# Bucket rows loaded transposed, expert rows added into the output by accumulating scatters

## The chip, the core and the metric

One core of a Trainium2 chip runs the whole kernel in one launch. The metric is the device time of that launch in microseconds (us).

## The reference

Block-wise causal attention (batch 8, 8 heads, 576 tokens, head size 64, blocks of 64), then a mixture of 8 experts with noisy top-2 routing over the 4608 tokens of 512 values. Cut to what matters:

```python
scores = np.where(block_i >= block_j, scale * q @ k.T, -1e9)
x = softmax(scores) @ v                       # (4608, 512)
noisy = x @ w_gate + log1p(exp(x @ w_noise)) * noise
top2_w = softmax(top 2 of noisy)              # per token
for e in range(8):
    for k in range(2):
        mask = top2[:, k] == e
        out[mask] += top2_w[mask, k, None] * (relu(x[mask] @ w1[e]) @ w2[e])
```

## The kernel before

Attention runs over four groups `g` of two batches, each nine row tiles of 128 tokens. For each group q and k are loaded and transposed on TensorE, scores and exponentials are made in two sets of four heads, and the result lands in `xr` (128 x 9 x 512, BF16). A router then finds each token's two experts and its place in their buckets. Two groups make a half; each half has its own bucket array `xd` in HBM, 8 experts x 640 rows, which a store from the tile `zero` clears at the start (unused rows must be finite). For each of the 72 pairs of row tile and choice, GpSimd scatters 128 rows of `xr` into `xd` at `slots`.

The expert stage takes 16 steps, half 0 and then half 1, experts 0 to 7 in each. `load_x` brings a bucket (640 x 512) into `xg` on SyncE's queue, two steps ahead. `expert` transposes it on TensorE into `xgT` (20 transposes and 4 VectorE copies), makes `hp` = w1 x `xgT` (64 matmuls), passes it through a Relu on ScalarE into `hsb`, makes `yp` = `hsb` x w2 in five row tiles (40 matmuls), copies each to `ysb` and stores it to `yd` in HBM. After the eighth and after the last step `combine` gathers, for each of 18 row tiles, the two expert rows of each token from `yd` (GpSimd, `gslots`), weighs and adds them (VectorE, `wts`) and stores to `out`.

Order: a framework places the instructions. Each engine gets its list in an order fixed before the run, by a model in which, of the instructions that are ready, the one that comes first in the program goes first; each tile waits for those that lay in its place. The second pool block lies over the first, in the order of its pools: `wL` (6 experts x 16 KB a partition), `xg`, `xgT`, `hsb` (2 x 10 KB), `ysb`, `fin`. In the first block `raw`, `qk`, `v` and the exponentials end at 124,448 bytes, and the two `xr` follow, to 142,880. Weights of experts 0 and 1 have a pool of their own; those of 2 to 7 are loaded into `wL` by GpSimd's queue.

After the last step a branch, not taken with this input, handles buckets that overflow.

Of the kernel before, what the change touches and what calls it, by code (L numbers as in the profile page):

```python
# [8 lines left out]
F32 = mybir.dt.float32  # L9
# [10 lines left out]
def kernel(  # L20
# [29 lines left out]
    NW = CAP // 2  # L50
    OVB = E * CAP
    XR = OVB + 2 * TH * P
    BIG = float(1 << 20)
    SET = 4
    EO = (0, 576, 1024, 1344)
    ESC = 1536
    scale = 1.0 / (D ** 0.5)

    xd = [nc.dram_tensor(f"xd{i}", (XR, Dm), BF16, kind="Internal").ap() for i in range(NH)]
    yd = [nc.dram_tensor(f"yd{i}", (OVB, Dm), BF16, kind="Internal").ap() for i in range(NH)]  # L60

# [25 lines left out]

    nz_all = keep.tile([P, NT, E], F32)
    slots = keep.tile([P, NT, 2], I32)
    gslots = keep.tile([P, NT, 2], I32)  # L90
    wts = keep.tile([P, 2, NT], F32)
    oh_all = keep.tile([P, NG, 2, E, TG], BF16)
    zero = keep.tile([P, 2048], BF16)

    def setup_consts():
        make_identity(nc, ident_f)
        nc.vector.tensor_copy(ident, ident_f)
        nc.gpsimd.memset(prem, 0.0)
        nc.gpsimd.affine_select(out=prem, in_=prem, compare_op=ALU.is_gt, fill=-1.0,
                                base=0, pattern=[[1, P]], channel_multiplier=-1)  # L100
        nc.vector.memset(ones_mat, 1.0)
        nc.gpsimd.iota(ecap_i, pattern=[[CAP, E], [0, 1]], base=0, channel_multiplier=0)
        nc.vector.tensor_copy(ecap, ecap_i)
        nc.vector.memset(rmask, 1.0)
        nc.vector.memset(rmask[:, :, 0:1], 0.0)
        nc.gpsimd.iota(ovrow_i, pattern=[[TH * P, 2], [P, TH]], base=OVB, channel_multiplier=1)
        nc.vector.tensor_copy(ovrow, ovrow_i)
        for i in range(NH):
            nc.vector.memset(base[i], 0.0)

    wload = {}

# [14 lines left out]
    with tc.tile_pool(name="raw", bufs=2) as raw_pool, \  # L127
# [59 lines left out]

        nc.vector.memset(zero, 0.0)
        for i in range(NH):
            zr = OVB // P  # L190
            nc.sync.dma_start(
                out=xd[i][0:OVB, :].rearrange("(p a) d -> p (a d)", p=P).rearrange("p (a c) -> p a c", c=2048),
                in_=zero.unsqueeze(1).to_broadcast([P, zr * Dm // 2048, 2048]))
# [8 lines left out]
        for g in range(NG):  # L202
# [12 lines left out]
                load_w(wE, 0)  # L215
                load_w(wE, 1)

            xr = xr_pool.tile([P, TG, Dm], BF16, tag="xr")
# [126 lines left out]
            for i in range(2):  # L345
# [4 lines left out]
            nc.vector.tensor_scalar(gslots[:, t0:t0 + TG, :].rearrange("p t i -> p i t"), sl2,  # L350
                                    float(OVB - 1), None, op0=ALU.min)
            nc.vector.tensor_copy(slots[:, t0:t0 + TG, :].rearrange("p t i -> p i t"), sl2)  # L352


            for idx in range(TG):
                for i in range(2):
                    ins = nc.gpsimd.indirect_dma_start(  # L357
                        out=xd[half], out_offset=bass.IndirectOffsetOnAxis(
                            ap=slots[:, t0 + idx, i:i + 1], axis=0),
                        in_=xr[:, idx, :], in_offset=None,  # L360
                        bounds_check=XR - 1, oob_is_err=False)
                    key = f"scat{half}"
                    tc.declare_no_dep(ins.ins, group=key, reason="rows of one half are distinct") if scat[half] else None
                    tc.add_to_no_dep_group(key, ins.ins)
                    scat[half].append(ins.ins.name)


    with tc.tile_pool(name="wL", bufs=1) as wL, \
         tc.tile_pool(name="xgp", bufs=3) as xg_pool, \
         tc.tile_pool(name="xgtp", bufs=2) as xgt_pool, \  # L370
# [5 lines left out]
         tc.tile_pool(name="ft_ps", bufs=2, space=PSUM) as ft_ps:  # L376

        def load_x(half, e):
            xg = xg_pool.tile([P, CT, Dm], BF16, tag="xg")
            ins = nc.sync.dma_start(out=xg, in_=xd[half][e * CAP:(e + 1) * CAP, :]  # L380
                                    .rearrange("(c p) d -> p c d", p=P))
            for nm in scat[half]:
                tc.add_manual_dep(ins.ins, nm, SYNC_DEP, reason="rows landed")
            return xg

        def expert(half, e, xg):
            w1sb, w2sb = wload[e]
            xgT = xgt_pool.tile([P, DB, CAP], BF16, tag="xgT")
            for db in range(DB):
                tp = ft_ps.tile([P, CAP], BF16, tag="ft")  # L390
                for c in range(CT):
                    nc.tensor.transpose(tp[:, c * P:(c + 1) * P], xg[:, c, db * P:(db + 1) * P], ident)  # L392
                nc.vector.tensor_copy(xgT[:, db, :], tp)  # L393
            hsb = h_pool.tile([P, FB, CAP], BF16, tag="hsb")
            for fb in range(FB):
                hp = hp_ps.tile([P, 2, 512], F32, tag="hp")
                for db in range(DB):
                    for n in range(2):
                        nc.tensor.matmul(out=hp[:, n, 0:NW], lhsT=w1sb[:, db, fb * P:(fb + 1) * P],  # L399
                                         rhs=xgT[:, db, n * NW:(n + 1) * NW],  # L400
                                         start=(db == 0), stop=(db == DB - 1))
                nc.scalar.activation(out=hsb[:, fb, :].rearrange("p (n w) -> p n w", n=2),  # L402
                                     in_=hp[:, :, 0:NW], func=AF.Relu)
            for c in range(CT):
                yp = yp_ps.tile([P, Dm], F32, tag="yp")
                for fb in range(FB):
                    nc.tensor.matmul(out=yp, lhsT=hsb[:, fb, c * P:(c + 1) * P], rhs=w2sb[:, fb, :],  # L407
                                     start=(fb == 0), stop=(fb == FB - 1))
                ysb = y_pool.tile([P, Dm], BF16, tag="ysb")
                nc.vector.tensor_copy(ysb, yp)  # L410
                nc.sync.dma_start(out=yd[half][e * CAP + c * P:e * CAP + (c + 1) * P, :], in_=ysb)

        def combine(half):
            for tl in range(TH):
                t = half * TH + tl
                g, idx = divmod(t, TG)
                yg = fin.tile([P, 2, Dm], BF16, tag="yg")
                for i in range(2):
                    nc.gpsimd.indirect_dma_start(  # L419
                        out=yg[:, i, :], out_offset=None, in_=yd[half],  # L420
                        in_offset=bass.IndirectOffsetOnAxis(ap=gslots[:, t, i:i + 1], axis=0),
                        bounds_check=OVB - 1, oob_is_err=False)
                acc = fin.tile([P, Dm], F32, tag="acc")
                nc.vector.tensor_scalar(acc, yg[:, 0, :], wts[:, 0, t:t + 1], None, op0=ALU.mult)  # L424
                nc.vector.scalar_tensor_tensor(out=acc, in0=yg[:, 1, :], scalar=wts[:, 1, t:t + 1], in1=acc,  # L425
                                               op0=ALU.mult, op1=ALU.add)
                for p0, n, tok in token_rows(g, idx):
                    nc.sync.dma_start(out=out[tok:tok + n, :], in_=acc[p0:p0 + n, :])

        seq = [(half, e) for half in range(NH) for e in range(E)]  # L430
        xgs = {0: load_x(*seq[0]), 1: load_x(*seq[1])}
        for e in range(2, E):
            load_w(wL, e)
        for i, (half, e) in enumerate(seq):
            if i + 2 < len(seq):
                xgs[i + 2] = load_x(*seq[i + 2])
            expert(half, e, xgs.pop(i))
            if i == E - 1:
                combine(0)
        combine(1)  # L440

# [10 lines left out]
        with tc.If(over > 0):  # L452
# [15 lines left out]
            for half in range(NH):  # L468
                with tc.For_i(half * TH * P, (half + 1) * TH * P, P) as r0:
# [4 lines left out]
                    xo = fin.tile([P, 2, Dm], BF16, tag="yg")  # L474
                    nc.gpsimd.indirect_dma_start(
                        out=xo[:, 0, :], out_offset=None, in_=xd[half],
                        in_offset=bass.IndirectOffsetOnAxis(ap=sidx, axis=0),
                        bounds_check=XR - 1, oob_is_err=False)
                    tp = ft_ps.tile([P, CAP], BF16, tag="ft")
                    for db in range(DB):  # L480
                        nc.tensor.transpose(tp[:, db * P:(db + 1) * P], xo[:, 0, db * P:(db + 1) * P], ident)
# [50 lines left out]
```

## Time and profile before

| | |
|---|---|
| median of 3 runs | 726.08 us (724.75 to 729.91) |
| profiled execution | 728.31 us, of which the span is 726.5 us |
| TensorE, share of the span | 65% (472.7 us) |
| VectorE, ScalarE, GpSimd | 35%, 26%, 30% |
| DMA | 91.62 MB, 102,902 packets |
| mean granted clock of TensorE | 0.785 of full speed |

A share of the span says little here, since the stages have different limits: loads at the start, attention, experts, combine. A stage is read by the stretch of time that it takes, and a wait by what released it. L399 in a row is line 399 of the kernel before. q0 is the DMA queue of GpSimd, q1 the queues of SyncE and ScalarE.

### The profile page before, as it was taken

To read this page: it belongs to the slowest core of one execution; us is meant where nothing else is said; L and a number is where in the kernel's file an instruction comes from. 1 tells how busy PE (TensorE), PEld (TensorE's weight loads), DVE (VectorE), ACT (ScalarE), POOL (GpSimd) and SP (SyncE) were. 2 spreads that over 40 slices of the span, in tenths; PEclk is the share of its full clock that TensorE was granted. 3 is DMA by queue.
4 is the path that set the end of the run, shared out by engine and by line. 5 is a ranking of instruction groups with operands and counts; after the bars stand their busy time and mean duration, and the time that the engine had idled before them with its cause. 6 is when DMAs were issued, how large, how long until landed. Compare 5 with 4: busy or idle time off the path is not lost.

```text
span 726.5 us, 10418 instructions
## 1 busy us (share of the span) xinstructions
PE 472.7 (65%) x4264; PEld 292.6 (40%) x4264; DVE 253.3 (35%) x591; ACT 187.3 (26%) x245; POOL 218.7 (30%) x244
## 2 busy tenths in 40 slices
PE   2087788361786284039999999964179999996000
PEld 1045446130563163025555555541055555553000
DVE  3054946150474155002222222235332222221443
ACT  0084480160415130013322222230033322221000
POOL 5126625777004413370000000077600000001773
PEclk9988866555566566559999999995589999999555
DMA  9999999492001209969942212256432221111564
GB/s 207 343 231 169 181 195 177 142 124 101 1 2 60 73 15 260 210 133 221 226 125 73 71 55 59 72 176 200 150 105 73 73 73 37 37 37 46 177 192 146
DMA packets 102902, 91.62 MB, mean 126 GB/s; under 512 B 49088, under 2 KB 86976, under 8 KB 102848
## 3 DMA queue, kind: packets, MB, share of 16 engines
q0 software_dynamic: 67744, 49.84, 45.8%
q1 hardware_dynamic: 35104, 41.05, 17.7%
q8 instruction: 35, 0.57, 0.3%
q14 instruction: 19, 0.16, 0.1%
HBM read 81.97 MB, written 39.85 MB: 168 GB/s over the span
## 4 chain that ended last, share of the span: by engine, by line
PE 50%; issue 12%; DMA 9%; another core or an unknown queue 9%; POOL 7%; DVE 7%; ACT 6%; POOLq 0%; DVEq 0%; ACTq 0%; SPq 0%
PE hp L399 18%; PE yp L407 18%; ACT esc L237 6%; POOL yg L419 4%; DMA kr<-in_k_dram 4%; PE av L261 4%; DMA vt<-in_v_dram 3%; PE sc L233 2%; PE av L275 2%; POOL xd L357 2%; PE tp L392 2%; PE tp L166 2%; DVE ysb L410 1%; PE tp L288 1%
## 5 line engine op out<-in xcount | busy, mean ns | idle before, releaser
L399 PE MATMUL hp<-xgT,w 128*128 128x320 bf16 x1024 | 149.9, 305 | 33.6 <-ACT hsb L402 33.6
L419 POOL DMA_INDIRECT yg<-yd,gslots x72 | 75.6, 1050 | 317.6 <-PE hp L399 149.4
L402 ACT ACTIVATE hsb<-hp 128x640 bf16<-128x640 f32 x128 | 89.9, 703 | 288.7 <-PE hp L399 246.6
L407 PE MATMUL yp<-w,hsb 128*128 128x512 bf16 x640 | 146.4, 388 | 17.8 <-DVE ysb L410 14.8
L399 PEld LDWEIGHTS <-w 128*128 128x128 bf16 x1024 | 101.5, 100 | 74.8 <-issue 34.0
L410 DVE CAST ysb<-yp 128x512 bf16<-128x512 f32 x80 | 55.3, 691 | 212.3 <-PE yp L407 203.3
L237 ACT ACTIVATE esc<-sc 128x1024 bf16<-128x1024 f32 x96 | 91.5, 1036 | 127.8 <-PE sc L233 72.2
L407 PEld LDWEIGHTS <-hsb 128*128 128x128 bf16 x640 | 63.5, 99 | 94.5 <-issue 24.5
L357 POOL DMA_INDIRECT xd<-xr,slots x72 | 71.0, 986 | 92.8 <-DVE slots L352 46.9
L233 PE MATMUL sc<-qT,kT 64*128 64x512 bf16 (+4 forms) x320 | 52.8, 376 | 29.4 <-ACT esc L237 27.4
L261 PE MATMUL av<-vt,esc 128*128 128x65 bf16 x640 | 42.6, 234 | 38.5 <-DVE xr L279 29.7
L261 PEld LDWEIGHTS <-esc 128*128 128x128 bf16 x640 | 34.4, 123 | 52.9 <-DVE xr L279 35.1
L155 POOL DMA_DIRECT2D vt<-in_v_dram x40 | 33.7, 867 | 53.6 <-DMA kr<-in_k_dram 14.2
L392 PE MATMUL tp<-ident,xg 128*128 128x128 bf16 x320 | 27.7, 233 | 28.5 <-DVE xgT L393 24.6
L393 DVE COPY xgT<-tp 128x640 bf16<-128x640 bf16 x64 | 29.0, 486 | 47.9 <-PE hp L399 44.8
L392 PEld LDWEIGHTS <-xg 128*128 128x128 bf16 x320 | 23.0, 105 | 35.8 <-DVE xgT L393 17.6
L278 DVE RECIPROCAL rden<-av 128x4 f32<-128x4 f32 x72 | 13.0, 182 | 68.1 <-remote 41.7
L166 PE MATMUL tp<-ident,qr 128*64 128x128 bf16 (+1 forms) x320 | 18.8, 274 | 27.2 <-DMA qr<-in_q_dram 14.8
L233 PEld LDWEIGHTS <-kT 64*128 64x128 bf16 x320 | 15.1, 102 | 51.5 <-issue 47.2
L172 DVE COPY qT<-tp 128x1024 bf16<-128x1024 bf16 (+1 forms) x20 | 22.3, 1117 | 33.8 <-PE tp L166 20.3
L425 DVE SCALAR_TENSOR_TENSOR acc<-yg,wts,acc 128x512 f32<-128x512 bf16 x36 | 26.5, 748 | 17.8 <-DMA yg<-yd,gslots 17.7
L424 DVE TENSOR_SCALAR acc<-yg,wts 128x512 f32<-128x512 bf16 x36 | 19.0, 529 | 35.8 <-DMA yg<-yd,gslots 31.1
(78 smaller groups left out, 278.9 us busy)
## 6 DMA issues: line engine op xcount, KB each, us to landing
w<-in_moe_w_dram POOLq DMA_DIRECT2D x16, 1024.0 KB
xd<-zero SPq DMA_DIRECT2D x2, 5120.0 KB
xg<-xd SPq DMA_DIRECT2D x16, 640.0 KB
yd<-ysb SPq DMA_DIRECT2D x80, 128.0 KB
out_dram<-acc SPq DMA_DIRECT2D x32, 256.0 KB
vt<-in_v_dram POOLq DMA_DIRECT2D x32, 128.0 KB
qr<-in_q_dram POOLq DMA_DIRECT2D x8, 384.0 KB
kr<-in_k_dram POOLq DMA_DIRECT2D x8, 384.0 KB
```

The lines of the kernel that those rows point to most:

```text
L155: nc.gpsimd.dma_start(out=vb[p0:p0 + n, idx, :, 0:D], in_=v[b, :, s0:s0 + n, :].rearrange("h s d -> s h d"))
L166: nc.tensor.transpose(tp[64 * hf:64 * hf + 64, r * n:(r + 1) * n], raw[p0:p0 + n, src_t, r * 64:(r + 1) * 64], ident[p0:p0 + n, p0:p0 + n])
L233: nc.tensor.matmul(out=sc[:, hf, off:off + z - a], lhsT=kT[sl, c0 + jt * P:c0 + jt * P + P], rhs=qT[sl, c0 + a:c0 + z], start=True, stop=True)
L237: nc.scalar.activation(out=esc[:, hh, :, u * 512:(u + 1) * 512], in_=sc, func=AF.Exp, scale=scale)
L261: nc.tensor.matmul(out=av[:, hh, :], lhsT=esc[:, hh, hf, c:c + P], rhs=vb[:, 4 * hf + jt, h, :], start=(jt == 0), stop=(jt == ib))
L357: ins = nc.gpsimd.indirect_dma_start(out=xd[half], out_offset=bass.IndirectOffsetOnAxis(ap=slots[:, t0 + idx, i:i + 1], axis=0), in_=xr[:, ...
L392: nc.tensor.transpose(tp[:, c * P:(c + 1) * P], xg[:, c, db * P:(db + 1) * P], ident)
L399: nc.tensor.matmul(out=hp[:, n, 0:NW], lhsT=w1sb[:, db, fb * P:(fb + 1) * P], rhs=xgT[:, db, n * NW:(n + 1) * NW], start=(db == 0), stop=( ...
L402: nc.scalar.activation(out=hsb[:, fb, :].rearrange("p (n w) -> p n w", n=2), in_=hp[:, :, 0:NW], func=AF.Relu)
L407: nc.tensor.matmul(out=yp, lhsT=hsb[:, fb, c * P:(c + 1) * P], rhs=w2sb[:, fb, :], start=(fb == 0), stop=(fb == FB - 1))
L410: nc.vector.tensor_copy(ysb, yp)
L419: nc.gpsimd.indirect_dma_start(out=yg[:, i, :], out_offset=None, in_=yd[half], in_offset=bass.IndirectOffsetOnAxis(ap=gslots[:, t, i:i + 1 ...
```

## The change

`load_x` loads each bucket transposed by the DMA itself, into a tile of the shape of `xgT`; the 20 transposes and the copies of `expert` are gone, and so is the pool of `xgT`. `yd`, `gslots` and `combine` are gone. Each bucket row has 8 more BF16 places, a record of four words: its slot, its token (as 8192 minus the token, so that an unused row, which is zero, points past the end), the second weight, and the first minus the second. `load_rec` reads the records of a half back, once, and makes of them for each bucket row the token number and the weight. `expert` scales each row of `yp` by its weight into an F32 `ysb` and adds it into `out` by an accumulating scatter from GpSimd; `out` is cleared by a store on ScalarE's queue. The first scatter of an expert waits for those of the expert before it, the other four don't.

```diff
+    DR = Dm + 8
+    TOKM = 8192
...
-    xd = [nc.dram_tensor(f"xd{i}", (XR, Dm), BF16, kind="Internal").ap() for i in range(NH)]
-    yd = [nc.dram_tensor(f"yd{i}", (OVB, Dm), BF16, kind="Internal").ap() for i in range(NH)]
+    xd = [nc.dram_tensor(f"xd{i}", (XR, DR), BF16, kind="Internal").ap() for i in range(NH)]
...
-    zero = keep.tile([P, 2048], BF16)
+    zero = keep.tile([P, 2080], BF16)
...
+            rec = xr[:, :, Dm:DR]
+            nc.vector.tensor_copy(rec[:, :, 0:2].bitcast(F32)[:, :, 0], sl2[:, 0, :])
+            nc.vector.tensor_copy(rec[:, :, 2:4].bitcast(I32)[:, :, 0], tokm[:, g, :])
+            nc.vector.tensor_copy(rec[:, :, 4:6].bitcast(F32)[:, :, 0], wk[:, 1, :])
+            nc.vector.tensor_tensor(out=rec[:, :, 6:8].bitcast(F32)[:, :, 0], in0=wk[:, 0, :],
+                                    in1=wk[:, 1, :], op=ALU.subtract)
...
         def load_x(half, e):
-            xg = xg_pool.tile([P, CT, Dm], BF16, tag="xg")
-            ins = nc.sync.dma_start(out=xg, in_=xd[half][e * CAP:(e + 1) * CAP, :]
-                                    .rearrange("(c p) d -> p c d", p=P))
+            xg = xg_pool.tile([P, DB, CAP], BF16, tag="xg")
+            ins = nc.sync.dma_start_transpose(out=xg, in_=xd[half][e * CAP:(e + 1) * CAP, 0:Dm])
...
-            xgT = xgt_pool.tile([P, DB, CAP], BF16, tag="xgT")
-            for db in range(DB):
-                tp = ft_ps.tile([P, CAP], BF16, tag="ft")
-                for c in range(CT):
-                    nc.tensor.transpose(tp[:, c * P:(c + 1) * P], xg[:, c, db * P:(db + 1) * P], ident)
-                nc.vector.tensor_copy(xgT[:, db, :], tp)
...
-                ysb = y_pool.tile([P, Dm], BF16, tag="ysb")
-                nc.vector.tensor_copy(ysb, yp)
-                nc.sync.dma_start(out=yd[half][e * CAP + c * P:e * CAP + (c + 1) * P, :], in_=ysb)
-
-        def combine(half):
...
+                ysb = y_pool.tile([P, Dm], F32, tag="ysb")
+                nc.vector.tensor_scalar(ysb, yp, wrow[half][:, e, c:c + 1], None, op0=ALU.mult)
+                ins = nc.gpsimd.indirect_dma_start(
+                    out=out, out_offset=bass.IndirectOffsetOnAxis(ap=trow[half][:, e, c:c + 1], axis=0),
+                    in_=ysb, in_offset=None, bounds_check=N - 1, oob_is_err=False, compute_op=ALU.add)
+                key = f"acc{half}_{e}"
+                if c:
+                    tc.declare_no_dep(ins.ins, group=key, reason="tokens of one expert are distinct")
+                tc.add_to_no_dep_group(key, ins.ins)
...
+        def load_rec(half):
+            rc = fin.tile([P, E, CT, 4], I32, tag="rc", bufs=1)
+            ins = nc.sync.dma_start(out=rc.rearrange("p e c w -> p (e c) w"),
+                                    in_=xd[half].bitcast(I32)[0:OVB, Dm // 2:DR // 2]
+                                    .rearrange("(c p) w -> p c w", p=P))
...
+            nc.vector.tensor_scalar(tr, f[1], -1.0, float(TOKM), op0=ALU.mult, op1=ALU.add)
...
         xgs = {0: load_x(*seq[0]), 1: load_x(*seq[1])}
+        load_rec(0)
+        zf = zero[:, 0:2048].bitcast(F32)
+        nc.scalar.dma_start(out=out.rearrange("(p a) d -> p (a d)", p=P).rearrange("p (a c) -> p a c", c=1024),
+                            in_=zf.unsqueeze(1).to_broadcast([P, N * Dm // P // 1024, 1024]))
         for e in range(2, E):
             load_w(wL, e)
...
             expert(half, e, xgs.pop(i))
-            if i == E - 1:
-                combine(0)
-        combine(1)
+            if i == 0:
+                load_rec(1)
```

## Rows read from the trace of the kernel before

**Rows 1.** The page, part 2, forty slices of 18.2 us: TensorE busy, granted clock

```profile
PE   2087788361786284039999999964179999996000
...
PEclk9988866555566566559999999995589999999555
```

**Rows 2.** Table of stretches: length, busy time of each engine, clock, DMA share, GB/s

```profile
0.00:35.00 35.00, 5.57 (x83) 3.91 (x83) 7.48 (x18) 1.28 (x1) 13.18 (x25) 1.00 1.00 271
35.00:57.00 22.00, 17.69 (x249) 10.38 (x251) 11.25 (x25) 17.19 (x19) 6.78 (x10) 0.84 1.98 230
...
290.00:320.00 30.00, 0.27 (x2) 0.16 (x2) 0.00 (x0) 1.03 (x2) 15.80 (x18) 0.50 0.72 171
...
375.00:471.00 96.00, 92.99 (x617) 56.28 (x615) 25.36 (x45) 28.13 (x40) 0.00 (x0) 1.00 0.22 69
471.00:532.00 61.00, 26.29 (x136) 14.01 (x136) 27.48 (x49) 5.62 (x8) 38.30 (x36) 0.68 0.56 177
...
667.00:726.50 59.50, 0.00 (x0) 0.00 (x0) 22.66 (x36) 0.00 (x0) 37.28 (x36) 0.53 0.52 162
```

**Rows 3.** The chain of waits at the start: start us, us, what

```profile
6.21 29.41 DMA kr<-in_k_dram
35.91 19.55 DMA vt<-in_v_dram
```

**Rows 4.** Timeline of one steady expert: start us, us, engine, line, operation

```profile
392.60 0.72 PE L392 MATMUL tp<-ident,xg 128*128 128x128 bf16 x10
392.80 0.69 DVE L410 CAST ysb<-yp 128x512 bf16<-128x512 f32 x1 [1.03 <-PE yp L407]
...
394.63 8.78 PE L399 MATMUL hp<-xgT,w 128*128 128x320 bf16 x63
...
403.25 8.80 PE L407 MATMUL yp<-w,hsb 128*128 128x512 bf16 x40
...
411.89 0.72 PE L392 MATMUL tp<-ident,xg 128*128 128x128 bf16 x10
```

**Rows 5.** Timeline where the expert stage starts; idle time and its releaser in brackets

```profile
298.49 0.98 POOL L357 DMA_INDIRECT xd<-xr,slots  x1 [5.53 <-DMA w<-in_moe_w_dram]
...
316.40 0.98 POOL L357 DMA_INDIRECT xd<-xr,slots  x1 [0.30 <-issue]
317.37 0.84 POOL L115 DMA_DIRECT2D w<-in_moe_w_dram  x1
...
318.97 1.30 ACT L402 ACTIVATE hsb<-hp 128x640 bf16<-128x640 f32 x2 [39.55 <-DMA xd<-xr,slots]
...
323.09 0.97 POOL L117 DMA_DIRECT2D w<-in_moe_w_dram  x1
```

**Rows 6.** DMA queues, 10 to 15 us: packets, MB, share of 16 engines

```profile
q1 hardware_dynamic: 330, 1.35, 70.7%
```

**Rows 7.** DMA queues, 278 to 280 us

```profile
q0 software_dynamic: 158, 0.32, 84.9%
q1 hardware_dynamic: 153, 0.16, 28.2%
```

**Rows 8.** DMA queues, 50 to 55 us: the noise loads

```profile
q1 hardware_dynamic: 1012, 0.03, 39.4%
```

**Rows 9.** DMA queues, 320 to 375 us: weights of experts 4 to 7

```profile
q0 software_dynamic: 6220, 8.28, 85.9%
```

**Rows 10.** DMA queues, 667 to 726 us: the gathers of the last combine

```profile
q0 software_dynamic: 1728, 4.72, 29.3%
```

**Rows 11.** Timeline, order of issue at the start and after the last router

```profile
0.75 3.25 SPq L200 DMA_DIRECT2D nz_all<-in_moe_noise_dram  x7
...
4.04 1.38 SPq L191 DMA_DIRECT2D xd<-zero  x2
...
283.95 0.23 DVE L446 TENSOR_REDUCE cmax<-base 128x1 f32<-128x8 f32 x2
```

**Rows 12.** Timeline, the last instruction of VectorE

```profile
719.56 0.75 DVE L425 SCALAR_TENSOR_TENSOR acc<-yg,wts,acc 128x512 f32<-128x512 bf16 x1 [1.30 <-DMA yg<-yd,gslots]
```

More of the change, by code (lines that the diff above doesn't have):

```diff
@@ L89 @@
     slots = keep.tile([P, NT, 2], I32)
-    gslots = keep.tile([P, NT, 2], I32)
     wts = keep.tile([P, 2, NT], F32)
+    tokm = consts.tile([P, NG, TG], I32)
+    rowid_i = consts.tile([P, E, CT], I32)
+    rowid = consts.tile([P, E, CT], F32)
     oh_all = keep.tile([P, NG, 2, E, TG], BF16)
-    zero = keep.tile([P, 2048], BF16)
+    zero = keep.tile([P, 2080], BF16)
     def setup_consts():
@@ L109, in setup_consts @@
             nc.vector.memset(base[i], 0.0)
+        nc.gpsimd.iota(tokm[:, :, 0:8].rearrange("p g (b t) -> p g b t", b=2),
+                       pattern=[[-2 * S, NG], [-S, 2], [-P, 4]], base=TOKM, channel_multiplier=-1)
+        for hf in range(2):
+            nc.gpsimd.iota(tokm[64 * hf:64 * hf + 64, :, 8:9], pattern=[[-2 * S, NG], [0, 1]],
+                           base=TOKM - 512 - hf * S, channel_multiplier=-1)
+        nc.gpsimd.iota(rowid_i, pattern=[[CAP, E], [P, CT]], base=0, channel_multiplier=1)
+        nc.vector.tensor_copy(rowid, rowid_i)
     wload = {}
@@ L189 @@
         for i in range(NH):
-            zr = OVB // P
             nc.sync.dma_start(
-                out=xd[i][0:OVB, :].rearrange("(p a) d -> p (a d)", p=P).rearrange("p (a c) -> p a c", c=2048),
-                in_=zero.unsqueeze(1).to_broadcast([P, zr * Dm // 2048, 2048]))
+                out=xd[i][0:OVB, :].rearrange("(p a) d -> p (a d)", p=P).rearrange("p (a c) -> p a c", c=2080),
+                in_=zero.unsqueeze(1).to_broadcast([P, OVB * DR // P // 2080, 2080]))
         load_v(0)
@@ L216 @@
                 load_w(wE, 1)
-            xr = xr_pool.tile([P, TG, Dm], BF16, tag="xr")
+            xr = xr_pool.tile([P, TG, DR], BF16, tag="xr")
             for st in range(H // SET):
@@ L349 @@
             nc.vector.tensor_tensor(out=sl2, in0=sl2, in1=ovrow[:, :, tl:tl + TG], op=ALU.min)
-            nc.vector.tensor_scalar(gslots[:, t0:t0 + TG, :].rearrange("p t i -> p i t"), sl2,
-                                    float(OVB - 1), None, op0=ALU.min)
             nc.vector.tensor_copy(slots[:, t0:t0 + TG, :].rearrange("p t i -> p i t"), sl2)
+            rec = xr[:, :, Dm:DR]
[4 more added lines that the diff above has]
+                                    in1=wk[:, 1, :], op=ALU.subtract)
             for idx in range(TG):
@@ L357 @@
                     ins = nc.gpsimd.indirect_dma_start(
-                        out=xd[half], out_offset=bass.IndirectOffsetOnAxis(
+                        out=xd[half].bitcast(I32), out_offset=bass.IndirectOffsetOnAxis(
                             ap=slots[:, t0 + idx, i:i + 1], axis=0),
-                        in_=xr[:, idx, :], in_offset=None,
+                        in_=xr[:, idx, :].bitcast(I32), in_offset=None,
                         bounds_check=XR - 1, oob_is_err=False)
@@ L369 @@
          tc.tile_pool(name="xgp", bufs=3) as xg_pool, \
-         tc.tile_pool(name="xgtp", bufs=2) as xgt_pool, \
          tc.tile_pool(name="hp", bufs=2) as h_pool, \
@@ L384, in load_x, with expert @@
             return xg
-        def expert(half, e, xg):
+        def expert(half, e, xgT):
             w1sb, w2sb = wload[e]
-            xgT = xgt_pool.tile([P, DB, CAP], BF16, tag="xgT")
-            for db in range(DB):
-                tp = ft_ps.tile([P, CAP], BF16, tag="ft")
-                for c in range(CT):
-                    nc.tensor.transpose(tp[:, c * P:(c + 1) * P], xg[:, c, db * P:(db + 1) * P], ident)
-                nc.vector.tensor_copy(xgT[:, db, :], tp)
             hsb = h_pool.tile([P, FB, CAP], BF16, tag="hsb")
@@ L408, in expert @@
                                      start=(fb == 0), stop=(fb == FB - 1))
-                ysb = y_pool.tile([P, Dm], BF16, tag="ysb")
-                nc.vector.tensor_copy(ysb, yp)
-                nc.sync.dma_start(out=yd[half][e * CAP + c * P:e * CAP + (c + 1) * P, :], in_=ysb)
-        def combine(half):
[L414 to L428, printed above, removed]
@@ new lines, in expert @@
+                tc.add_to_no_dep_group(key, ins.ins)
+        wrow, trow = {}, {}
+        def load_rec(half):
[3 more added lines that the diff above has]
+                                    .rearrange("(c p) w -> p c w", p=P))
+            for nm in scat[half]:
+                tc.add_manual_dep(ins.ins, nm, SYNC_DEP, reason="rows landed")
+            f = [rc[:, :, :, i].bitcast(I32 if i == 1 else F32) for i in range(4)]
+            tr = keep.tile([P, E, CT], I32, name=f"trow{half}")
+            nc.vector.tensor_scalar(tr, f[1], -1.0, float(TOKM), op0=ALU.mult, op1=ALU.add)
+            wr = keep.tile([P, E, CT], F32, name=f"wrow{half}")
+            nc.vector.tensor_tensor(out=wr, in0=f[0], in1=rowid, op=ALU.is_equal)
+            nc.vector.tensor_tensor(out=wr, in0=wr, in1=f[3], op=ALU.mult)
+            nc.vector.tensor_tensor(out=wr, in0=wr, in1=f[2], op=ALU.add)
+            trow[half], wrow[half] = tr, wr
@@ L473 @@
                     nc.sync.dma_start(out=wrow, in_=tok_w[bass.ds(r0, P), :])
-                    xo = fin.tile([P, 2, Dm], BF16, tag="yg")
+                    xo = fin.tile([P, DR], BF16, tag="xo")
                     nc.gpsimd.indirect_dma_start(
-                        out=xo[:, 0, :], out_offset=None, in_=xd[half],
+                        out=xo, out_offset=None, in_=xd[half],
                         in_offset=bass.IndirectOffsetOnAxis(ap=sidx, axis=0),
@@ L480 @@
                     for db in range(DB):
-                        nc.tensor.transpose(tp[:, db * P:(db + 1) * P], xo[:, 0, db * P:(db + 1) * P], ident)
+                        nc.tensor.transpose(tp[:, db * P:(db + 1) * P], xo[:, db * P:(db + 1) * P], ident)
                     xoT = y_pool.tile([P, DB, P], BF16, tag="ysb")
```

## The prediction, made before the changed kernel ran

> **What bounds the kernel now.** I read the slices first, then a table of stretches, then the chain of waits, and last the timeline of one expert. The slices show TensorE busy in two blocks of nines (slices 18 to 25 and 30 to 35, counted from 0) with a hole between them, an empty tail of three slices, and an uneven first half at a low clock [rows 1]. The stretches put numbers on that: two blocks in which TensorE is the limit, a hole from 471 to 532 with 26 us of matmul in 61, and a tail of 59.5 us with none [rows 2]. In the hole and in the tail GpSimd issues gathers (36 each time [rows 2]) and VectorE weighs and adds rows. The start is bound otherwise: the chain's first 55 us are two DMA waits, for k and for v [rows 3], with the DMA share at 1.00 and above [rows 2]. So there are three kinds of stage: loads (to 57), attention (to 270), experts (to 667, with the hole) and the last combine.
>
> In a steady expert the first matmuls take 403.25 - 394.63 = 8.62 us, the second ones 411.89 - 403.25 = 8.64 us, and the period is 411.89 - 392.60 = 19.29 us [rows 4]. The missing 2.03 us are the 20 transposes and the copies that they wait for.
>
> **Transposes and yd stores go.** Without transposes an expert costs 8.62 + 8.64 = 17.26 us. Nothing else is late in that period: ScalarE's copies and VectorE's copy from PSUM (0.69 us of every 1.73 [rows 4]) have slack, and the scaled F32 copy reads the same PSUM tile; I price it the same. What the removed work covered is the next load: it is hidden only if it lands within a period (below).
>
> **The hole and the tail go.** No combine stands between experts 7 and 8 any more, so expert 8 costs a period instead of 60 us. At the end there remains one copy (0.7 us), one scatter issue (1.0 us [rows 5]), its landing (2.4 us, taken from the last scatter of before, issued at 316.40, on which the work at 318.97 waits [rows 5]) and the program's end. Today 6.2 us lie between the end of the last add, 720.3, and the end of the span, store included [rows 12]. I take 9 us for all of it.
>
> **The zero fill of the output comes.** 4608 x 512 F32 is 9.44 MB, 2304 pieces of 4 KB. The fill of xd, of the same size of piece, shows the price: 330 packets held 70.7% of 16 engines for 5 us, so 0.707 x 5 x 16 / 330 = 0.171 us each [rows 6], and 2304 x 0.171 / 16 = 24.6 us of all engines. Where does it fall? It stands late in the program on ScalarE's queue, but instructions do not run in program order: the noise loads went out ahead of the fill that precedes them, and a reduction from the program's very end (line 446) ran straight after the last router [rows 11]. The fill needs only the zeroed tile, and ScalarE idles at the start; so I expect it in the first microseconds, against the loads of q, k and v that the chain waits on. Queues share the engines packet by packet (158 and 153 packets of two queues in the same 2 us [rows 7]), so a third queue hides nothing there: all of the 24.6 us moves the end of v, and attention with it. The Trainium skill, in DMA: Bandwidth & Descriptors, "Issuing engines are not separate DMA queues", says the same, that another issuing engine saves sequencer time only; reading the idle ScalarE queue as free would make this term 0. If the fill runs at its place in the program instead, it shares the engines with the weights at 270 to 303 and delays the last scatters by as much.
>
> **Buckets grow by a record.** Rows of 1040 instead of 1024 bytes add 1.6% to the fill and to 72 scatters, and four small VectorE operations per group replace one: under 1 us on the path. The record loads are 5120 pieces of 16 bytes per half. The noise loads (32 bytes) show 0.394 x 5 x 16 / 1012 = 0.031 us a packet [rows 8], so 5120 x 0.031 / 16 = 9.9 us of the engines each.
>
> **Where the expert stage starts.** Today the first matmul waits until 319: its hsb buffer lies over the last group's xr, which the scatters still read (39.6 us of wait on them [rows 5]). After the change xgT's pool is gone and the first hsb buffer ends below xr; the y pool (6 x 2 KB) lies there. So expert 0's first matmuls and two of its five second ones come free, and its first copy out waits for the scatters instead. These scatters end at 318.8 today; with the fill and a record load sharing the engines I take 345.
>
> **What the accumulating scatters queue behind.** Weights of experts 4 to 7, eight loads, are issued on GpSimd from 317.37 to 324, right behind the scatters [rows 5], and keep the engines for 0.859 x 55 = 47 us [rows 9]. GpSimd's DMAs have one queue, served in order: scatters of the last group already waited 5.5 us for weights ahead of them [rows 5]. Today GpSimd has nothing else until 471 [rows 2]. After the change every y row leaves by that queue. Expert 0's five scatters and so five of six y buffers stay behind the weights; expert 1 finds one buffer and two PSUM tiles, then TensorE stands, and with it VectorE's queue. The weights end at 345 + 47 + 10 (the second record load, sharing packet by packet) + 3 (bucket loads) = 405, the first scatter lands near 408. Then two products of expert 1 (3.5 us) and 14 experts remain: 408 + 3.5 + 14 x 17.26 = 653; with the tail 662, and with the 1.8 us that lie around the span 664. The profiled execution took 728.31, 2.2 us more than the median, so the forecast against the median is 662.
>
> **Prices that no row has.** A transposing load moves 640 KB in 256-byte pieces if it works on 128 columns at once: 2560 pieces. Low end: today's plain load, 640 packets at 0.282 x 2 x 16 / 153 = 0.059 us [rows 7], 2.4 us. High end: each piece costs as much as such a 1 KB packet, 9.4 us. I take the smallest packet's 0.031 us, 5.0 us, nearest in size. The Trainium skill (same page, "Latency and other measured facts") gives 261 GB/s for one measured transposing DMA; an estimate from it is 2.5 us, and the load would be hidden with more room. No row here shows it. An accumulating scatter moves 256 KB. Today's gathers moved 4.72 MB in 0.293 x 59 = 17.3 us of the engines [rows 10], 0.96 us for 256 KB; low end once that, high end three times (both reads and the write one after another), 2.9 us. I take twice, 1.9 us, since a store that reads first does at least two transfers. A period then needs 5 x 1.9 + 5.0 = 14.5 us of DMA: under 17.26. At both high ends it needs 23.9.
>
> **Rivals.**
> *A: no standstill behind the weights.* If scatters don't wait for the weights (another order on GpSimd), the stage runs from 345 without a pause: 0.7 + 5.2 (three products) + 15 x 17.26 give 610, with tail and rim 621, against the median 619. For it: where GpSimd's issues stand is decided by readiness [rows 11]. Against: the eight loads are ready before any y row.
> *B: the DMA engines set the pace (slower).* With both prices at the high end a period is 23.9 us: 411.5 + 14 x 23.9 + 9 + 1.8 = 757. It decides from a period of (728.3 - 10.8 - 411.5) / 14 = 21.9 us; between 17.26 and that it only eats gain. A transposing load that goes element by element instead of in pieces would be the extreme: then the change doesn't do what it says. Against: these engines are 22% busy in a steady expert today [rows 2].
> *C: the fill costs nothing,* because it fits into a gap of the DMA: 24.6 us less, 637. Against: the share is full up to 57 us [rows 2], and again from 270.
>
> **How the numbers follow.** Forecast 0.45 (645 to 685: the ends of landing, record loads and restart of the clock, which is near half speed in every gap [rows 1]); A 0.22 (600 to 640); C 0.10; B 0.23, of which 0.13 end below 719, 0.02 within 1%, 0.08 above 733. One per cent is about what a measurement of this kernel can tell from no change. Faster 0.90, same 0.02, slower 0.08. The range takes in A's upper half and B's lower cases: 610 to 705.
>
> **What would show it.** Right: xd's and the output's fill both in flight in the first 60 us, v landing near 80 instead of 55; no L392 and no gathers; hp after yp without a gap, a period of 17.3; expert 1's copies held until the weights are in, one idle stretch of TensorE of some 40 us near 365 to 408; a tail under 12 us. Wrong: the fill elsewhere; bucket loads that TensorE waits for in every period (B); scatters landing late in every period, with GpSimd waiting for the previous expert's last one before the next expert's first (B); TensorE running through 365 to 408 (A).

## The result, and the profile after

The changed kernel takes 681.87 us (median of 4 runs, 680.1 to 684.4), the kernel before on the same chip 727.52: a ratio of 0.938 (95% interval 0.933 to 0.943). The forecast was 662 with a range of 610 to 705. The profiled execution took 681.86 with a span of 680.0. Where the runs of one kernel spread by more than 1.5%, its ratio goes by the fast ones alone, those within 1.5% of the lowest (of the kernels below only c_lateonly). The slices of the profile's page (TensorE, granted clock), each 17 us long; they answer to [rows 1]:

```profile
PE   1105777400872676174207039999999999999993
...
PEclk9999778855685588556657559999999999999997
```

One block of nines to the end in place of two, and no tail. But there are two deep zeros ahead of it: slices 8 and 9 in the middle of attention, and a ragged stretch from slice 18 to 23. The stretches (busy time of PE, PEld, DVE, ACT, POOL, then clock, DMA share, GB/s), to be laid beside [rows 2]:

```profile
35.00:57.00 22.00, 2.31 (x33) 1.78 (x34) 1.37 (x2) 0.00 (x0) 2.62 (x3) 1.00 1.07 373
57.00:76.00 19.00, 14.99 (x172) 8.56 (x169) 8.99 (x19) 14.45 (x16) 3.81 (x6) 0.73 2.03 253
...
130.00:170.00 40.00, 0.00 (x0) 0.00 (x0) 0.00 (x0) 0.89 (x1) 25.79 (x30) 0.50 1.29 152
170.00:312.00 142.00, 88.40 (x1296) 61.06 (x1296) 68.77 (x211) 48.24 (x59) 43.83 (x46) 0.62 0.29 46
...
361.00:403.00 42.00, 13.68 (x68) 7.55 (x68) 2.19 (x6) 5.23 (x8) 5.84 (x8) 0.62 1.29 199
403.00:670.00 267.00, 266.16 (x1581) 154.89 (x1579) 58.58 (x78) 84.36 (x120) 121.73 (x79) 0.99 0.70 106
670.00:680.00 10.00, 0.00 (x0) 0.00 (x0) 0.00 (x0) 0.00 (x0) 1.96 (x2) 0.64 0.39 57
```

What fills 35 to 57 before fills 57 to 76 now: TensorE's first instructions that wait for v start at 78.88 us instead of 55.50, 23.4 later. Then comes a stretch of 40 us in which neither TensorE nor VectorE does anything, which nothing in the prediction provides for. From 403 on TensorE is busy for 266.16 of 267 us. The timeline says what stood in the way, in brackets the idle time before an instruction and what ended it:

```profile
2.98 0.63 ACTq L447 DMA_DIRECT2D out_dram<-zero  x1
...
170.23 0.17 DVE L363 COPY xr<-tokm 128x9 int32<-128x9 int32 x1 [44.62 <-DMA xd<-xr,slots]
...
170.85 0.46 PE L270 MATMUL av<-vt,esc 128*128 128x65 bf16 x5 [41.34 <-DVE esc L260]
...
311.74 35.44 SPq L393 DMA_TRANSPOSE xg<-xd  x3
...
360.72 1.30 ACT L408 ACTIVATE hsb<-hp 128x640 bf16<-128x640 f32 x2 [42.02 <-DMA xd<-xr,slots]
361.47 3.89 PE L405 MATMUL hp<-xg,w 128*128 128x320 bf16 x14 [29.91 <-ACT hsb L408]
...
399.60 0.20 DVE L436 TENSOR_SCALAR trow<-rc 128x40 int32<-128x40 int32 x1 [42.40 <-DMA rc<-xd]
...
401.43 3.14 PE L413 MATMUL yp<-w,hsb 128*128 128x512 bf16 x7 [27.85 <-DVE ysb L416]
...
409.09 8.86 PE L405 MATMUL hp<-xg,w 128*128 128x320 bf16 x64
417.79 8.80 PE L413 MATMUL yp<-w,hsb 128*128 128x512 bf16 x40
426.42 8.86 PE L405 MATMUL hp<-xg,w 128*128 128x320 bf16 x64
...
670.72 1.55 POOL L417 DMA_INDIRECT out_dram<-ysb,trow  x1 [0.30 <-DVEq L468]
```

Read it from the top. The output's fill goes out at 2.98 us, as forecast. A copy of nine words per partition (L363, the token numbers of group 2, into the xr buffer of group 0) stands on VectorE for 44.6 us, since the scatters still read the buffer that it writes; the masks of attention (L260) stand behind it on VectorE's list, and TensorE behind them. Group 0's slots are ready at 114.9, but its 18 scatters are issued from 145.42 to 168.36, behind loads of v and k on GpSimd's list, four of which wait for loads of weights. The first hsb waits for the scatters, as before the change [rows 5]. Then expert 0's second products wait 27.9 us for VectorE, which itself waits 42.4 us for the second record load. The period after that is 426.42 - 409.09 = 17.33 us.

Expert 0 has another such place. Its first matmuls wait for the first bucket load, and on TensorE's list the last group's router (L337, L338) stands behind them. The first lines are of the kernel before, the others of the changed one:

```profile
269.72 12.45 SPq L380 DMA_DIRECT2D xg<-xd  x5
274.35 1.99 PE L392 MATMUL tp<-ident,xg 128*128 128x128 bf16 x15 [0.61 <-DMA xg<-xd]
...
327.05 3.62 PE L405 MATMUL hp<-xg,w 128*128 128x320 bf16 x13 [11.64 <-DMA xg<-xd]
330.83 0.30 DVE L340 TENSOR_TENSOR_SCAN incl<-rmask,pp 128x72 f32<-128x72 f32 x1 [11.94 <-PE pp L338]
```

The plain load was in 4.6 us after its issue, the transposing one took 15.3 us here beside the weights of experts 2 and 3 (in the steady stage its median is 4.5). The scatters show no loss by it in this stage: those of the last group begin 21.9 us after the first bucket load instead of 14.5 (b_after against c_before, below), but no longer wait for weights in between, and end 44.8 us after it instead of 47.6.

Split at the first bucket load, the account is short. Before, it came at 269.7, now at 311.7: attention lost 42.0 us. From there to the span's end it was 726.5 - 269.7 = 456.8 us and is 680.0 - 311.7 = 368.3: the expert stage gained 88.5.

### The profile page after: what moved, and what is told of

It is laid out like the page before. It is cut to its first block, busy times and chain, and to the rows that moved or that the text cites. A ratio compares the mean times of both kernels' runs of the same rounds, so it can differ in the third digit from the quotient of the medians.

```text
span 680.0 us, 9421 instructions
## 1 busy us (share of the span) xinstructions
PE 437.3 (64%) x3944; PEld 268.1 (39%) x3944; DVE 189.2 (28%) x476; ACT 187.0 (28%) x245; POOL 267.6 (39%) x256
## 5 line engine op out<-in xcount | busy, mean ns | idle before, releaser
L417 POOL DMA_INDIRECT out_dram<-ysb,trow x80 | 123.9, 1548 | 178.6 <-DVE ysb L416 159.4
L405 PE MATMUL hp<-xg,w 128*128 128x320 bf16 x1024 | 146.0, 304 | 41.6 <-ACT hsb L408 29.9
L413 PE MATMUL yp<-w,hsb 128*128 128x512 bf16 x640 | 143.4, 384 | 27.9 <-DVE ysb L416 27.9
L416 DVE TENSOR_SCALAR ysb<-yp,wrow 128x512 f32<-128x512 f32 x80 | 60.0, 751 | 209.5 <-PE yp L413 209.3
L270 PE MATMUL av<-vt,esc 128*128 128x65 bf16 x640 | 41.7, 232 | 77.0 <-DVE esc L260 41.3
L242 PE MATMUL sc<-qT,kT 64*128 64x512 bf16 (+4 forms) x320 | 49.0, 356 | 24.8 <-ACT esc L246 23.9
L176 PE MATMUL tp<-ident,qr 128*64 128x128 bf16 (+1 forms) x320 | 17.4, 260 | 39.8 <-DMA qr<-in_q_dram 27.9
L242 PEld LDWEIGHTS <-kT 64*128 64x128 bf16 x320 | 14.9, 100 | 45.4 <-issue 41.0
L176 PEld LDWEIGHTS <-qr 128*64 128x64 bf16 (+1 forms) x320 | 13.7, 138 | 44.2 <-DMA qr<-in_q_dram 37.1
L288 DVE TENSOR_TENSOR xr<-av,rden 128x256 bf16<-128x256 f32 x72 | 28.5, 415 | 1.1
L176 PE MATMUL tp<-ident,kr 128*64 128x128 bf16 (+1 forms) x320 | 17.1, 255 | 17.6 <-DMA kr<-in_k_dram 13.4
L182 DVE COPY kT<-tp 128x1024 bf16<-128x1024 bf16 (+1 forms) x20 | 22.5, 1126 | 13.2 <-PE tp L176 13.1
L176 PEld LDWEIGHTS <-kr 128*64 128x64 bf16 (+1 forms) x320 | 14.1, 137 | 20.1 <-DMA kr<-in_k_dram 13.9
```

Of the source, the lines that this page charges most:

```text
L176: nc.tensor.transpose(tp[64 * hf:64 * hf + 64, r * n:(r + 1) * n], raw[p0:p0 + n, src_t, r * 64:(r + 1) * 64], ident[p0:p0 + n, p0:p0 + n])
L182: nc.vector.tensor_copy(dv, pv)
L242: nc.tensor.matmul(out=sc[:, hf, off:off + z - a], lhsT=kT[sl, c0 + jt * P:c0 + jt * P + P], rhs=qT[sl, c0 + a:c0 + z], start=True, stop=True)
L270: nc.tensor.matmul(out=av[:, hh, :], lhsT=esc[:, hh, hf, c:c + P], rhs=vb[:, 4 * hf + jt, h, :], start=(jt == 0), stop=(jt == ib))
L416: nc.vector.tensor_scalar(ysb, yp, wrow[half][:, e, c:c + 1], None, op0=ALU.mult)
L417: ins = nc.gpsimd.indirect_dma_start(out=out, out_offset=bass.IndirectOffsetOnAxis(ap=trow[half][:, e, c:c + 1], axis=0), in_=ysb, in_offs ...
```

## The experiments

They ran on three other chips, one for each first letter, on which the kernel before takes 668 to 669 us. So the unedited change was run there too, and each ratio is against the kernel before on its own chip.

**c_before**, the kernel before, for its profile there (one execution):

> The kernel before, for a profile on the chip of the experiments, where it takes 669 us and not 727.5. Theory: attention ends near 219 us here as in the run with the transposing loads alone, not at 270, and the waits that the trace of before gives to no engine of its core (48.8 us for ScalarE's exponentials, 41.7 us for VectorE's reciprocals) are not there; the experts take the same 19.3 us a period. Rival: the experts or the combine differ too.

It took 672.8 us. Its first bucket load comes at 216.9 us and no wait is put down to "remote" any more. On the first chip the view of waits, grouped, has these four and a fifth of 2.2 us (us in total, times, longest; waits of several engines can lie over each other):

```profile
ACT esc L237 <- remote: 48.8, 5, 14.6
DVE rden L278 <- remote: 41.7, 6, 13.3
DVE ysb L410 <- remote: 9.0, 1, 9.0
DVE kT L172 <- remote: 5.7, 1, 5.7
```

The rest is alike: from the bucket load to the end 670.9 - 216.9 = 454.0 us against 456.8. So all but 3 us of the difference between the two chips lies in attention, as expected. What "remote" stands for stays open.

**b_after**, the change unedited:

> The changed kernel as it is, as the base line of this group. The kernel before took 727.5 us on one chip and 668.8 us on the chip of the first group of experiments. My theory: what the change does is the same on both chips, and the first experiments that left its attention stage alone took 651 us there; so if this chip is like the second one, about 652 us and a ratio near 0.975, with the second token copy waiting some 45 us for the first group's scatters and VectorE some 44 us for the second record load. Rival: the ratio is that of the first chip, 0.938, so 627 us; then the experiments with 651 us were slower than the changed kernel.

649.04 us, ratio 0.969 (0.965 to 0.972). Expert stage 647.4 - 282.5 = 364.9 us, 89.1 less than c_before, where the first chip gave 88.5. This was the theory. Attention ends 282.5 - 216.9 = 65.6 us later. That is more than the 42.0 of the first chip. Part of it can be seen: here the token copy of group 3 waits as well, 13.9 us, and on the first chip it doesn't; and there the "remote" waits of the changed kernel come to 66 us instead of 107, all of them after 207 us, where before they begin at 121. That the new waits lay over the "remote" ones there is still argued, not shown.

**a_tok**: the token word no longer becomes ready before the router, since it is made from the router's slots (times zero).

```diff
-nc.vector.tensor_copy(rec[...][:, :, 0], tokm[:, g, :])
+nc.vector.scalar_tensor_tensor(out=rec[...][:, :, 0], in0=sl2[:, 0, :],
+    scalar=0.0, in1=tokm[:, g, :], op0=ALU.mult, op1=ALU.add)
```

> The token word of each row is written from the router's last result (times zero, plus the token), so that it can't go ahead of it on VectorE; nothing else moves. Theory: the copy of group 2's tokens stands before the exponentials' clearing on VectorE's list and waits 44.6 us for group 0's scatters, and TensorE behind it 41.3 us; without it the first bucket load is issued some 20 us earlier than 311.7 (about 290) and the time falls to about 660. Rival: the attention stage is longer only because the loads come later after the fill, and the wait is then taken over by the first use of the same buffer; time 677 to 684, first bucket load at 308 or later.

606.53 us, ratio 0.907 (0.902 to 0.911); first bucket load at 239.5, 43 us earlier than in b_after: the theory, at twice the 20 us it gave. Group 2's copy and the first bucket load in b_after, then here:

```profile
172.00 0.17 DVE L363 COPY xr<-tokm 128x9 int32<-128x9 int32 x1 [44.99 <-DMA xd<-xr,slots]
282.50 31.27 SPq L393 DMA_TRANSPOSE xg<-xd  x3
...
161.97 0.17 DVE L363 SCALAR_TENSOR_TENSOR xr<-sl,tokm 128x9 int32<-128x9 f32 x1
239.48 31.57 SPq L393 DMA_TRANSPOSE xg<-xd  x3
```

In b_after TensorE stands 41.5 and 10.4 us behind the copies of groups 2 and 3; here its longest wait between 100 and 239 us is 6.4. One small instruction's place on VectorE's list is worth twice what the whole change gains on these chips.

**a_fill**: the zeros of the output are made from group 2's kT (times zero), so that the fill goes out in mid attention.

```diff
+nc.vector.tensor_scalar(zf, kT[:, 0:1024], 0.0, None, op0=ALU.mult)
 nc.scalar.dma_start(out=out..., in_=zf...)
```

> The output is cleared in the middle of attention (the source tile is made from group 2's transposed k times zero) instead of in the first microseconds. Theory: the fill took 24.6 us of all DMA engines at the start, v ended at 76 instead of 55.5, and all of that shift goes through; with the fill at about 190 us, where the engines are mostly idle, v ends near 56 and the time is about 660. Rival: a later wait (on group 0's scatters) ends at the same time anyway, and the time moves by less than 7 us.

641.81 us, ratio 0.957 (0.953 to 0.961). The bucket load comes 7 us earlier, not 20 or 25, which is near the rival, because the token copy still waits (45.4 us). With that copy out of the way as well (b_all, below) the fill's move is worth 239.5 - 222.2 = 17.3 us. Taken in this order, the 65.6 us of attention are 43 for the copies, 17.3 for the fill, and 5.3 for all else.

**a_rec**: the second record load waits for expert 5's copies, and VectorE's operations on it stand behind those.

```diff
-if i == 0: load_rec(1)
+if i == 5: load_rec(1, copies[-3])
```

> The second half's record load waits for a copy out of expert 5, so VectorE's list has its four operations there and not before expert 0's copies. Theory from the trace of the changed kernel: VectorE stood from 357 to 399.6 for that load, which shares the engines packet by packet with the weights of experts 4 to 7, and TensorE for 28 us with it; without it expert 0's copies go at about 372. By that theory alone the time falls by 25 to 28 us, to about 655. The prediction's own theory (scatters of y rows queue behind those weights and hold the six y buffers): TensorE stops again in expert 1 until the weights are in, near 395 (10 us earlier, since the record load no longer shares with them), and the time falls by 5 to 12 us, to 670 to 677.

651.25 us, ratio 0.972 (0.968 to 0.976): nothing gained, less than either theory gave. Its timeline shows why:

```profile
370.77 1.54 POOL L417 DMA_INDIRECT out_dram<-ysb,trow  x1 [3.95 <-DMA w<-in_moe_w_dram]
389.90 0.75 DVE L416 TENSOR_SCALAR ysb<-yp,wrow 128x512 f32<-128x512 f32 x1 [31.26 <-DMA out_dram<-ysb,trow]
390.70 5.75 PE L413 MATMUL yp<-w,hsb 128*128 128x512 bf16 x16 [29.40 <-DVE ysb L416]
```

With the record load moved away, TensorE stands 29.4 us for a y buffer, whose scatter sits behind the weights of experts 4 to 7 on GpSimd's queue, in expert 1: the prediction's mechanism, hidden behind the other wait in the change as it is. It ends 390.7 - 283.5 = 107.2 us after the first bucket load.

**a_tile**: waits buffer by buffer, not pool by pool, for hsb and ysb (one execution).

```diff
-tc.tile_pool(name="hp", bufs=2)
+tc.tile_pool(name="hp", bufs=2, reuse_waits="tile")
```

> The pools of hsb and ysb wait tile by tile for what lay in their place instead of pool by pool; the order of the instructions is the same. Theory: the first hsb buffer does not lie over xr, so expert 0's first matmuls run through from 331 instead of standing 29.9 us for the scatters, but its copies still wait for the record load until about 399.6, so the time stays within 4 us of the changed kernel's 682. Rival: the start of the expert stage sets the end, and the time falls by 8 us or more.

651.18 us. ScalarE's wait for the scatters is gone and expert 0's first products run through from 298 us, where b_after stops in them until 330, as the prediction had assumed; then TensorE stands 58.4 us for VectorE and the second record load instead of 27.3. A stall ahead of a later stall cost nothing here.

**b_trans**, the transposing loads alone (before, with L380's load transposed and lines L388 to L393 out):

> The kernel before with the transposing loads alone: no TensorE transposes, no xgT, the rest as before (yd stores, gathers, plain bucket rows of 1024 bytes, no fill of the output). My theory: a period falls from 19.3 to 17.3 us, the load (2560 pieces at 0.019 us, 3 us of the engines) is hidden, and the hole and the tail of gathers stay: 15 to 16 experts x 2.03 = 30 to 32 us less than before, a ratio near 0.955. Rival 1: beside stores and gathers the transposing load lands later than a period, or the waits for its row loads at the stage's start grow; then within 1% of before. Rival 2: with TensorE faster the hole of gathers between the halves grows by what the first half gains, so only half, 16 us, is left (0.976).

643.80 us, ratio 0.961 (0.957 to 0.964): 25.3 us less than before, where 30 to 32 were expected, and 5 less than both parts together. The period is 17.33 us.

**b_acc**, the accumulating scatters alone (after, with plain loads and TensorE transposes):

> The changed kernel with plain loads and TensorE transposes put back, so the accumulating scatters alone; to make room, the buffers of the overflow branch, which does not run, are fewer. My theory: the period is 19.3 us again and the start of the stage is the same, set by the weights and the second record load, so 14 x 2.03 = 28 us more than the changed kernel of this group. Rival: the 2 us a period vanish in some wait that the longer period hides, so less than 10 us more.

686.58 us, ratio 1.027 (1.024 to 1.030): slower than before. Against b_after it is 37.5 us more, as the theory had it: 14 periods of 19.35 instead of 17.33 (28), and expert 0's second products go on at 378.4 instead of 369.8 (8.6). The copies of groups 2 and 3 wait here too (44.4 and 14.0 us), so what is slower is this way of writing the part, not accumulating scatters as such.

**b_all**: the edits of a_tok, a_fill, a_rec and a_tile together.

> All four edits of the first group at once: the token word made from the router's slots, the output cleared from a late tile, the second record load after a copy of expert 5, and waits taken buffer by buffer for hsb and yp instead of for the whole pools. In the first group the token word alone gave 606.5 us where the kernel before takes 668.8. My theory: the first bucket load starts near 231 us (239.5 less 8 by the fill), the y rows come at once, and then the y buffers fill up behind the scatters and the weights, as the second record load no longer does it first; the weights are in some 106 us after the first bucket load, as in the run with the later record load, so 337 + 3 + 14 x 17.3 + 10 = 592 us. Rival: without the waits on whole pools and on the record load nothing holds TensorE, and it is 231 + 10 + 16 x 17.3 + 10 = 528 to 560 us.

586.32 us, ratio 0.875 (0.873 to 0.877), the best of the runs with c_late, and near the theory's 592. Of the 62.7 us below b_after, 60.3 lie ahead of the first bucket load; the expert stage is 585.9 - 222.2 = 363.7 us, as good as unchanged. TensorE stands three times on the way: for the first bucket load, in expert 0 for its copies (VectorE has the first record load only at 265.6, then waits 4.3 us for the last group's scatters), and in expert 1 as in a_rec:

```profile
236.63 3.62 PE L412 MATMUL hp<-xg,w 128*128 128x320 bf16 x13 [10.50 <-DMA xg<-xd]
...
271.60 6.99 PE L420 MATMUL yp<-w,hsb 128*128 128x512 bf16 x24 [20.56 <-DVE ysb L423]
...
324.98 0.75 DVE L423 TENSOR_SCALAR ysb<-yp,wrow 128x512 f32<-128x512 f32 x1 [35.19 <-DMA out_dram<-ysb,trow]
325.79 5.47 PE L420 MATMUL yp<-w,hsb 128*128 128x512 bf16 x16 [33.33 <-DVE ysb L423]
```

**c_late** and **c_lateonly**: the weights of expert e (4 to 7) are loaded after the third copy of expert e - 4, on top of b_all and on the change alone.

```diff
-for e in range(2, E): load_w(wL, e)
+for e in range(2, 4): load_w(wL, e)
...
 expert(half, e, xgs.pop(i))
+if i + 4 < E: load_w(wL, i + 4, copies[-3])
```

> The version with all four edits of the second group (586.3 us, before 669.1), and the weights of experts 4 to 7 loaded one expert at a time as in the run before. There TensorE still stands 33.3 us for a y buffer whose scatter waits behind those weights. My theory: the 33 us go, 553 us. Rival: the weights' 47 us of engines come back as four waits of some 8 us, or as late bucket loads: 575 to 585 us.

584.50 us, ratio 0.878 (0.873 to 0.884), the same as b_all: the rival was right. The standing of 33.3 us is gone; in its place are five waits of 2.5 to 6.8 us between 331 and 394. GpSimd's issues show where they come from:

```profile
328.64 1.56 POOL L133 DMA_DIRECT2D w<-in_moe_w_dram  x1
351.45 1.58 POOL L427 DMA_INDIRECT out_dram<-ysb,trow  x1 [21.25 <-DVE ysb L426]
...
360.76 1.56 POOL L133 DMA_DIRECT2D w<-in_moe_w_dram  x1
381.71 1.58 POOL L427 DMA_INDIRECT out_dram<-ysb,trow  x1 [19.39 <-DVE ysb L426]
```

An expert with a weight load behind its scatters takes 30 us (381.71 - 351.45).

> The changed kernel with one edit: the weights of experts 4 to 7 are each loaded after the third copy of the expert four before, instead of straight after the last scatters. In the base line of the second group (649.0 us, before 669.1) TensorE stands 27.3 us in expert 0, while VectorE waits 44.4 us for the second record load, which shares the engines with these weights; with that load moved away (a_rec) it stood 29.4 us for y buffers behind the same weights. My theory: both waits are the weights', so both go at once, and nothing else fills the hole: 649 - 27 = 622 us, a ratio near 0.93. Rival: the record load, 5120 pieces of 16 bytes, is slow by itself, or the accumulating scatters wait for the weights in each of four periods instead of once: then 640 to 650 us, the sum of the waits being the same.

666.03 us, ratio 0.988 (0.983 to 0.993), with runs from 653.7 to 675.7: by the ratios 2% slower than the unedited change, and slower than the rival too. In the profiled execution, of 665.4 us, VectorE's wait for the second record load is 17.2 us instead of 44.4 and TensorE no longer waits on it, but VectorE waits 76 us for y buffers, in 13 waits; the longest leaves TensorE idle for 25.2 us, in the middle of the stage. My theory fell: the weights' time on the queue is not saved by spreading it. Why the runs spread so far stays open.

**c_ally**: b_all with 11 y buffers instead of 6.

> The version with all four edits of the second group, and 11 buffers for y rows instead of 6 (the buffers of the overflow branch, which does not run, are fewer). If the standstill is y buffers behind the weights, five more let TensorE go on for one expert more: 586.3 - 17 = 569 us. Rival: the scatters that are held back come in one burst behind the weights and TensorE stands later for as long: within 5 us of 586.

628.07 us, ratio 0.940 (0.935 to 0.945), 42 us worse than b_all, by neither theory:

```profile
203.37 0.20 DVE L443 TENSOR_SCALAR trow<-rc 128x40 int32<-128x40 int32 x1 [62.48 <-DMA rc<-xd]
204.66 0.84 PE L277 MATMUL av<-vt,esc 128*128 128x65 bf16 x12 [62.78 <-DVE esc L267]
```

VectorE's first use of the first record load now stands in the middle of attention and stops it for 62 us, the a_tok trap with another instruction. The expert stage itself did gain: 627.5 - 276.3 = 351.2 us, 12.5 less than b_all, near the 17 that were expected; TensorE's last standstill is 18.9 us instead of 33.3 and comes one expert later.

## Why the prediction was right, and which steps were not

The gains were right: the period, the hole and the tail. On those rests that the total came out inside the range. The expert stage was put at 662 - (269.7 + 24.6) = 367.7 us from the first bucket load to the span's end and measured 368.3, and that close an agreement is luck, since two misses cancel. The standstill was to end 408 - 294.3 = 113.7 us after the first bucket load, with 254 us of work and tail behind it; it ended 401.4 - 311.7 = 89.7 us after it, 24 earlier, but already in expert 0, so that 680.0 - 401.4 = 278.6 us were left. What remains of the miss, 680.0 - 662 = 18 us, is attention: 42.0 us where 24.6 were forecast.

There is luck in the chip as well. As a ratio the forecast is 662 / 726.08 = 0.912, with 0.971 at the range's end. On the first chip 0.938 was measured, on that of b_after 0.969, where the waits that the forecast lacked cost more.

- *Transposes gone, 17.26 a period:* right (17.33), no gap between an expert's two products. b_trans has the same period with that part alone.
- *Transposing load and accumulating scatter:* 5.0 and 1.9 us of engines were taken. The view of DMA for one period of the changed kernel, 500 to 517.3 us:

```profile
q0 software_dynamic: 715, 1.16, 49.7%
q1 hardware_dynamic: 2592, 0.66, 17.6%
```

  2592 packets, so 256-byte pieces as assumed, and 0.176 x 17.3 = 3.0 us; five scatters 0.497 x 17.3 = 8.6, so 1.7 each. Together 11.6 us a period, far from the 21.9 at which B decides. The issue costs GpSimd 1.55 us a scatter, not 1.0, harmless at five a period. The load took 15.3 us at the stage's start, where the forecast has no term for it. What the Trainium skill would have given for the load, an estimate of 2.5 us (DMA: Bandwidth & Descriptors, "Latency and other measured facts"), is nearer to the 3.0 measured than the 5.0 taken.
- *Tail 9 us:* nearly right; the last copy out of PSUM starts at 669.2, the span ends at 680, 10.8 us later.
- *Zero fill, 24.6 us at the start:* place right, and nearly the size: v comes 23.4 us later. That all of it moves attention's end is wrong: 17.3 us in b_all against a_tok. That it is not free (C) holds.
- *"Four small VectorE operations per group replace one: under 1 us on the path":* the step that failed. Their busy time is that small, but one of them needs only a free buffer, so it was put early on VectorE's list, where it waits for scatters. a_tok shows it: 43 us on the chips of the experiments. On the first chip TensorE stands 41.3 us for it, and attention ends 17.4 us later than forecast. The prediction had even read that readiness sets the order [rows 11] and used it for the fill alone.
- *"The first hsb buffer ends below xr":* the address is right, but the first products wait all the same (29.9 us); a_tile shows that waits on whole pools do it, and that they cost nothing here.
- *The standstill until about 408:* it ended at 401.4, close on the clock only by the two misses above, and its first cause was not the one forecast. VectorE waits 42.4 us for the second record load, priced at 9.9 us of engines but in only 38.9 us after its issue as it shares the engines with the weights packet by packet: 1536 and 1535 packets of the two queues from 370 to 380 us. The y buffers behind the weights are the next wait and as long: a_rec has them where the prediction had, in expert 1, ending 107.2 us after the first bucket load, where the forecast without its 10 us for the record load gives 103.7. So A needs both gone, and the one other order on the queue that was run (c_late) doesn't do it.

In b_all TensorE's three waits come to 64.4 us between the first bucket load and 326 us. What would be left of that stretch without them is only argued: scatters of the last group, weights and y rows share one queue, whatever their order. Weights on another queue weren't tried, nor a first bucket load that comes sooner.

## What to carry to other kernels

Price a small instruction by what it waits for and what is behind it on its engine, not by its busy time: look for any that becomes ready early and writes a buffer that a DMA still reads, or reads what a DMA still brings. When a wait is removed, expect the next of about the same length, and compare stages from a common mark (here the first bucket load) before crediting an edit. A change of two parts is worth running as two: here one part alone beat both together, and the other alone was slower than before. And when a total agrees, lay its terms beside the trace one by one: here two misses of 24 us hid in one stage.

## What was not expected of the hardware

- The same kernel took 727.5 us on one chip and 668 to 669 on three others, all but 3 us of the difference in attention; the first chip's trace has 107 us of waits, summed over engines, that it gives to no engine of the core, the one of the others has none.
- A record load of 80 KB in 16-byte pieces lands 5.5 us after its issue when it comes late (c_late, the second; 9.3 in b_all) and 38.9 us after it beside the weights of experts 4 to 7 (the change, on either chip). The transposing bucket load, in 256-byte pieces, takes 15.3 us beside weights and 4.5 (median) in the steady stage.
- An accumulating scatter occupies GpSimd for 1.55 us where the plain scatter takes 0.98, and the engines for 1.7 us.
